# Block-sparse attention with a fused MLP: picked block numbers loaded one block at a time, and a new order table

## The chip, the cores and the metric

The kernel runs on one core of one Trainium2 chip. The metric is the device time of one execution in microseconds. TensorE multiplies matrices, VectorE (DVE) and ScalarE (ACT) do elementwise work, GpSimd (POOL) some of that and the indirect gathers, and SyncE (SP) issues most of the DMA transfers.

## The reference, cut to what matters

Block-sparse attention over 4 batches of 8 heads, 768 positions of 64 dimensions, in blocks of 32. A query block sees the blocks beside it, the first and the last block, and three blocks that an input picks for it. The attention output goes through a two-layer MLP.

```python
mask = np.abs(blk_i - blk_j) <= window
mask = mask | (blk_i == 0) | (blk_j == 0) | (blk_i == n_blocks - 1) | (blk_j == n_blocks - 1)
for qb in range(n_blocks):
    for kb in sampled_blocks[qb]:
        mask[qb * block:(qb + 1) * block, kb * block:(kb + 1) * block] = True
scores = np.where(mask, scores, -1000000000.0)
...
h = x @ w_in
relu6 = np.clip(h + 3.0, 0.0, 6.0)
g = h * relu6 / 6.0
return (g @ w_out).astype(np.float32)
```

## The kernel before, in words

**Units.** The attention is cut into 28 units, u0 to u27; a unit is four query blocks of one batch, for all eight heads. Its steps: `q` loads the queries; `keys` loads the eight key blocks of one query block (five neighbours in one transfer, three picked ones in one each); `values` loads four neighbours' values; `gather` fetches the picked values (an indirect DMA on GpSimd with the row numbers of the tile `rows`, or four plain transfers on SP). `s` (halves 0 and 1) makes scores on TensorE, `r_` reads them on VectorE with bias and row minimum, `e` is the exponential on ScalarE, `t` the transposes on TensorE, `c` copies them out of PSUM, `a` is the product with the values, `n_` the division on VectorE, `x` a transpose, and `xh` and `xl` split the result into a rounded part (ScalarE) and its residue (VectorE). The units of batch 0 that come first, u0 to u2, have their keys already on the chip (`keys0` of k0 loads a whole batch): for them `chosen` copies the three picked key blocks of one query block, with a picked number in a register as the address. The other units' `keys` and SP's `gather` take the numbers from registers of SP.

**MLP.** Three units make a chunk of 384 rows; eight chunks with 16 steps each are the steps m0 to m127. A step's `h` is twelve matmuls, `ga` and `gb` (ScalarE, VectorE) the activation, `gh` and `gl` its rounded part and residue, and `o0` to `o2` three matmuls each. 32 weight tiles w0 to w31 come in as 512 KB of 64-bit words each and are turned into float32 by `size`, `low` (ScalarE or another), `sign` and `bits` (VectorE), then split by `hi` and `lo` into rounded part and residue, again for every chunk. Nine buffers take the raw words; `load` into one waits for the `bits` of the weight that was there before.

**Order.** The order of everything is written out in a table, SCORE: every phrase names a unit, weight or step, and the operations to be issued next; a letter behind a point names the engine (d VectorE, a ScalarE, p GpSimd, s SP). Each engine runs its own operations strictly in that order, and so does SP with its transfers: a transfer whose buffer is not yet free holds up those behind it.

**The registers.** `registers` (line 383) loads, on the engine that asks, all 16 picked numbers of a unit at its first `chosen` (or `keys`) in one instruction, and the unit keeps them for that engine. The numbers lie in the tile `picked`, which VectorE clamps at the start. k0's `place` on TensorE and `rows` on VectorE make the gathers' row numbers; `flag`, `spread` and `bias` make the mask's bias.

Of the kernel before, what the change touches and what calls it, by code (L numbers as in the profile page):

```python
# [61 lines left out]
w11 bits; m4 ga; w15 load6; w16 size; m5 h; w12 bits; m3 gh.a; m4 gb; w5 hi.p; w7 hi.a; w12 hi.a; w13 sign; u4 keys0; w16 low.a; u3 s0; w5 lo.d; w12
lo.d; m2 o0; w14 low.a; u3 r_00; m3 gl.p; m6 h; w14 size; u3 r_01; u4 values0; w13 bits; u3 e00; w18 load0; u3 e01 r_02; w7 lo.p; m5 ga; u3 r_03 s1
e02; w22 load4; m5 gb; u3 e03; w14 sign; w20 load2; m2 o1; w15 size; u3 r_10; w15 low.p; w17 size; m3 o0; u3 r_11 e10; w14 bits; u4 keys2; m2 o2; u3
e11 r_12; w17 low.p; m3 o1; w14 hi.a; u3 r_13; m4 gh.a; u3 t00; w14 lo.d; w9 hi.a; u3 t01 t10; m4 gl.d; u3 e13; u5 q; m3 o2; u3 c01.a; w9 lo.d; u4
values1; u3 c10.a; m7 h; w21 load3; w15 sign; m6 ga; w16 sign; w11 hi.a; u3 e12; m6 gb; w19 load1; m5 gh.p; u3 c00.a; m4 o0; w16 bits; w18 size; u4
keys3; u3 t11; m5 gl.d; w16 hi.a; m4 o1; w15 bits; m7 ga; u3 c11.a; m4 o2; w16 lo.d; w20 size; m7 gb; u3 a; w11 lo.p; w13 hi.a; w20 low.a; w13 lo.d;
w22 size; m8 h; u4 keys1; u3 d; u4 gather3.p; w19 size; w17 sign; w21 low.a; u3 n_; w18 low.p; w22 low.a; m5 o0; w17 bits; u4 gather2.p; w19 low.a; u5
keys0; u3 x; m6 gh.d; w21 size; m5 o1; w20 sign; u5 gather0.p; u3 xh; m6 gl.d; m5 o2; u3 xl; m8 ga; u5 gather1.p; m6 o0; w20 bits; m7 gh.a; w15 hi.a;
m6 o1; m8 gb; u4 values2; m7 gl.d; u4 values3 s0; w25 load2; w15 lo.d; m6 o2; w18 sign; u5 values1; u4 r_00; m7 o0; m8 gh.a; w18 bits; u4 e00; u5  # L70
keys1; m7 o1; u4 r_01; w17 hi.a; m8 gl.d; u4 e01; m7 o2; u4 r_02; w17 lo.p; w18 hi.a; u4 r_03 t00 e02 s1 e03; w22 sign; w23 load0; u5 values0; u4
c00.a; w18 lo.d; m8 o0; w20 hi.a; u4 r_10; w25 low.p size; u4 t01 r_11; u6 q; m8 o1; u4 e10; w20 lo.d; u4 e11; m9 h; u4 r_12 c01.a; w22 bits; u4 e12;
u5 keys2; u4 r_13; w21 sign; u4 e13 t10; w23 size; w19 sign; m10 h; w22 hi.a; u4 d; w26 load4; u4 c10.a; w19 bits; m9 ga; w22 lo.d; w24 load1; w19
hi.a; u4 t11; m9 gb; m8 o2; m10 ga; w23 low.p; u4 c11.a; m10 gb; m11 h; m9 gh.a; w19 lo.d; m10 gh.a; w23 sign; u5 keys3; m9 gl.d; u4 a; w23 bits; m11
ga; w26 size; w21 bits; w26 low.a; m11 gb; w27 load0; w21 hi.p; m9 o0; u5 values2; u4 n_; w24 size; u5 values3 gather2.p; w24 low.a; w21 lo.d; u4 x;
m9 o1; m10 gl.d; u4 xh; u5 gather3.p; w24 sign; m10 o0; u4 xl; m9 o2; u6 gather2.p keys3; w24 bits; u5 s0; m11 gh.a; w25 sign; w23 hi.a; u6 gather3.p;
m10 o1; m11 gl.d; w24 hi.a; u5 r_00; w27 size; m10 o2; w24 lo.d; u5 e00; w28 load1; u5 r_01; w27 low.p; m12 h; u5 e01 r_02; w23 lo.d; u5 e02 r_03; w25
bits; u5 e03 s1; m12 ga; w26 sign; w29 load2; u6 keys2; m11 o0; m12 gb; w25 hi.p; u5 r_10; m12 gh.a; u5 t00; w25 lo.d; m11 o1; u5 e10 r_11 c00.a; m12
gl.p; m11 o2; w28 size; u5 r_12; u6 values3; w26 bits; u5 e11 t01; u6 values2; m12 o0; u5 e12 r_13; w28 low.p; w26 hi.a; u5 t10; w27 sign; u5 e13; m12
o1; u5 c01.a; w26 lo.d; u5 t11 c10.a; m12 o2; w27 bits; u5 c11.a; m13 h; w29 size; u5 d; w30 load0; w27 hi.a; w28 sign; w27 lo.d; u5 a; w28 bits; m13  # L80
ga; w29 low.d; w28 hi.a; w31 load1; m13 gb; w28 lo.d; u6 s0; m13 gh.a; u8 gather0.p; u6 values4; w30 low.a; u5 n_; m14 h; m13 gl.d; w30 size; u6 r_00;
w30 sign; u6 e00 r_01; w31 size; w30 bits; u5 x; u6 e01; m13 o0; u6 r_02; u5 xh; w31 sign; u6 t00; w30 hi.a; m13 o1; u6 r_03; w0 hi.a; w30 lo.d; m14
ga; m13 o2; u5 xl; u6 e02; m15 h; u6 c00.a; w0 lo.d; u6 e03; m14 gb; w29 sign; m14 gh.a; w31 low.d; m16 h; m15 ga; w29 bits; u8 keys2; w2 hi.a; m15
gb; w29 hi.a; w2 lo.d; m15 gh.a; u6 s1; w31 bits; w4 hi.a; m14 gl.d; w31 hi.a; u7 values5; m17 h; u6 r_10; w29 lo.p; m16 ga; u7 values6; u6 r_11 e10;
m16 gb; u6 e11 r_12; m14 o0; m15 gl.d; w6 hi.a; u6 r_13 e12 t01; u9 keys0; w31 lo.d; u6 t10; m17 ga; m14 o1; w4 lo.d; u6 e13; m15 o0; u6 c01.a; m17
gb; u6 c10.a; w6 lo.d; u6 t11; m15 oc0.a o1; u8 q; u6 d c11.a; u8 values0; m14 o2; m15 oc1.d od0; m19 h; m16 gh.a; m15 od1; w1 hi.a; m16 gl.d; w1
lo.p; m15 o2; u9 keys1; m16 o0; m17 gh.a; w3 hi.a; m18 h; m17 gl.d; w3 lo.p; m15 oc2.d; u8 keys0; m17 o0; m18 ga; m19 ga; m16 o1; m18 gb; w8 hi.a; w10
hi.p; m19 gb; u6 a; w8 lo.d; w10 lo.d; m15 od2; m17 o1; u6 n_; u8 gather2.p values3 values1; m16 o2; u8 values2 gather3.p; m21 h; u8 keys3; w5 hi.a;
m18 gh.a; w5 lo.d; u8 gather1.p; m18 gl.d; m17 o2; m20 h; w7 hi.a; m19 gh.a; w7 lo.d; m19 gl.d; u8 keys1; m18 o0; m20 ga; w12 hi.p; w14 hi.a; u7 s0;
# [688 lines left out]
```

## Time and profile before

| | |
|---|---|
| three runs | 779.84 us median (779.8 to 781.73) |
| profiled execution | 779.34 us; its span, from the first to the last instruction, is 777.6 us |
| mean granted TensorE clock | 0.995 |
| busy: TensorE, VectorE, ScalarE, GpSimd | 754.0, 520.9, 406.5, 187.3 us |
| DMA | 119.53 MB moved, mean 154 GB/s |

Times in the profile count from the first instruction of the span. Nearly all operations go through one helper, line 242, so a row is told apart by its tiles (output <- inputs) and its time. "Busy" of TensorE is modelled from pipelined matmuls. An idle time in front of an instruction is put down to what ended it; "issue" means that the profile shows nothing that the engine waited for.

### The profile page before, as it was taken

To read this page: it belongs to the slowest core of one execution; us is meant where nothing else is said; L and a number is where in the kernel's file an instruction comes from. 1 tells how busy PE (TensorE), PEld (TensorE's weight loads), DVE (VectorE), ACT (ScalarE), POOL (GpSimd) and SP (SyncE) were. 2 spreads that over 40 slices of the span, in tenths; PEclk is the share of its full clock that TensorE was granted. 3 is DMA by queue.
4 is the path that set the end of the run, shared out by engine and by line. 5 is a ranking of instruction groups with operands and counts; after the bars stand their busy time and mean duration, and the time that the engine had idled before them with its cause. 6 is when DMAs were issued, how large, how long until landed. Compare 5 with 4: busy or idle time off the path is not lost.

```text
span 777.6 us, 22739 instructions
## 1 busy us (share of the span) xinstructions
PE 754.0 (97%) x9078; PEld 649.8 (84%) x9078; DVE 520.9 (67%) x1304; ACT 406.5 (52%) x996; POOL 187.3 (24%) x200
## 2 busy tenths in 40 slices
PE   5789999999999999999999999999999999999996
PEld 5679887888888888898888888888888898889985
DVE  2568988955565665565656666767777677676763
ACT  2677977847555656455656553343543522452122
POOL 4531434141332221102123004222013511300110
PEclk9999999999999999999999999999999999999999
DMA  9949997660464673147245517464145670201001
GB/s 325 392 171 305 297 301 262 195 211 15 151 184 118 180 234 117 42 122 215 70 143 179 168 43 225 170 185 145 62 148 141 206 255 2 83 3 41 0 1 41
DMA packets 79687, 119.53 MB, mean 154 GB/s; under 512 B 10018, under 2 KB 45990, under 8 KB 79582
## 3 DMA queue, kind: packets, MB, share of 16 engines
q1 hardware_dynamic: 72674, 96.18, 38.6%
q0 software_dynamic: 6640, 21.76, 8.9%
q8 instruction: 72, 1.18, 0.6%
q14 instruction: 33, 0.27, 0.1%
q10 hardware_dynamic: 268, 0.14, 0.1%
...
## 4 chain that ended last, share of the span: by engine, by line
PE 89%; DVE 1%; DMA 0%; issue 0%; ACT 0%; ACTq 0%
PE out L242 35%; PE h L242 33%; PE att L242 21%; DMA out_dram<-ot 0%; DVE wout L242 0%; DVE wlo_in L242 0%; DVE wlo_out L242 0%; ACT ot L242 0%; DVE g L242 0%; DVE win L242 0%; ACTq L242 0%
## 5 line engine op out<-in xcount | busy, mean ns | idle before, releaser
L242 PE MATMUL h<-x,whi_in 128*128 128x384 f32 x1024 | 265.1, 339 | 1.7 <-ACT x L242 1.4
L242 PEld LDWEIGHTS h<-x,whi_in 128*128 128x128 f32 x1024 | 186.9, 189 | 12.3 <-ACT x L242 1.6
L242 PE MATMUL h<-x,wlo_in 128*128 128x384 f32 x512 | 172.9, 338 | 0.3 <-DVE wlo_in L242 0.3
L242 PE MATMUL out<-whi_out,ghi 128*128 128x512 f32 x384 | 162.2, 422 | 0.0
L242 ACT ACTIVATE p<-p,m 128x256 f32<-128x256 f32 x224 | 112.6, 504 | 83.8 <-DVE m L242 82.9
L242 PE MATMUL out<-whi_out,glo 128*128 128x512 f32 x384 | 151.6, 395 | 0.0
L242 PE MATMUL out<-wlo_out,ghi 128*128 128x512 f32 x384 | 151.1, 394 | 0.0
L242 ACT ACTIVATE g<-h,half_b 128x384 f32<-128x384 f32 x128 | 73.0, 580 | 149.2 <-PE h L242 131.6
L242 POOL DMA_INDIRECT vr<-vB,rows x77 | 76.9, 999 | 167.9 <-PE att L242 145.7
L242 DVE SCALAR_TENSOR_TENSOR g<-g,h 128x384 f32<-128x384 f32 x128 | 69.7, 551 | 57.8 <-ACT g L242 57.2
L242 PEld LDWEIGHTS h<-x,wlo_in 128*128 128x128 f32 x512 | 96.5, 188 | 0.6 <-DVE wlo_in L242 0.6
L242 PEld LDWEIGHTS out<-whi_out,ghi 128*128 128x128 f32 x384 | 72.2, 188 | 22.3 <-issue 12.3
L242 DVE TENSOR_TENSOR wlo_out<-wout,whi_out 128x512 fp32r<-128x512 f32 x106 | 76.1, 718 | 21.9 <-ACT whi_out L242 18.9
L242 DVE TENSOR_TENSOR wlo_in<-win,whi_in 128x512 fp32r<-128x512 f32 x107 | 75.2, 704 | 21.0 <-ACT whi_in L242 18.4
L242 DVE CUSTOM_DVE_ANT_1 p<-att,bias 128x256 f32<-128x256 f32 x176 | 68.6, 419 | 25.8 <-PE att L242 25.5
L242 PEld LDWEIGHTS out<-whi_out,glo 128*128 128x128 f32 x384 | 72.1, 188 | 16.3
L242 PEld LDWEIGHTS out<-wlo_out,ghi 128*128 128x128 f32 x384 | 72.5, 189 | 7.7
L242 DVE TENSOR_TENSOR glo<-g,ghi 128x384 fp32r<-128x384 f32 x114 | 67.9, 596 | 14.2 <-ACT ghi L242 12.0
L242 POOL TENSOR_TENSOR wlo_in<-win,whi_in 128x512 fp32r<-128x512 f32 x21 | 27.8, 1322 | 160.1 <-DVE whi_in L242 105.5
L242 ACT CAST ghi<-g 128x384 fp32r<-128x384 f32 x94 | 47.9, 512 | 32.1 <-PE out L242 29.4
L242 ACT COPY pt<-att 128x512 f32<-128x512 f32 x89 | 51.0, 586 | 24.6 <-PE att L242 23.7
L242 PE MATMUL att<-kr,q 64*32 64x256 f32 (+1 forms) x1280 | 59.7, 376 | 0.7 <-issue 0.7
...
## 6 DMA issues: line engine op xcount, KB each, us to landing
...
```

What stands on the lines that cost most here:

```text
L242: self.last = tc.keep_in_program_order(op(*a, **k)).ins
```

## The change

`registers` on an engine other than SP now loads the three numbers of one query block alone and keeps them with that block; SP still loads 16 for a unit. A new operation `numbers` does this load by itself, and the new table has twelve of them, all right behind the clamp: nine on ScalarE, three on VectorE. All twelve `chosen` remain; nine are on ScalarE and three on VectorE (before: four each on ScalarE, VectorE and GpSimd).

The table itself is made anew. It has the same operations otherwise, in another order, and some on other engines. Counts before and after: `hi` on ScalarE 127 and 256, on VectorE 112 and 0, on GpSimd 17 and 0; `lo` on VectorE 213 and 255, on GpSimd 43 and 1; `gh` on ScalarE 94 and 126, on VectorE 24 and 0, on GpSimd 10 and 2; `gl` on VectorE 114 and 99, on GpSimd 14 and 29; `c` on ScalarE 95 and 62, on VectorE 17 and 50; `oc` on ScalarE 13 and 24, on VectorE 11 and 0; `low` on ScalarE 18 and 28, on VectorE 4 and 2, on GpSimd 10 and 2; `gather` on GpSimd 83 and 82, on SP 5 and 6. `place` stands behind u0.s0 and no longer ahead of `spread`. The diff, the table cut to the part up to the first MLP steps:

```diff
 SCORE = """
-k0 load keys0; u0 q values1 values0 values2 values3; k0 clamp folding number flag; u0 chosen2.a; u1 q; u0 chosen0.p; k0 place; u1 values1 values0; u0
-chosen1.a chosen3.p; u1 values3 values2; k0 rows; u1 chosen0.p; k0 spread; u2 values1 values0; u1 chosen1.d; u0 gather0.p s0; u2 values3; k0 bias; u0
-gather2.p; w4 load4; u0 s1 r_00; w1 load1; u0 gather1.p e00 r_01; u2 values2; u0 e01 r_02; w0 load0; u0 gather3.p e02 r_03 t00 r_10; u2 q; u1
-chosen3.a; u2 chosen1.d; u1 gather1.p; w2 load2; u0 c00.a r_11; w3 load3; u0 e10 r_12; u1 chosen2.p; u0 e11 r_13 e12; u1 gather3.p; w6 load6; u2
-chosen0.d; u1 s0; u0 e03 e13; u1 gather0.p; u0 d t01; u1 r_00; w4 size; u0 t10; u1 gather2.p; w4 low.d; u1 e00; u0 t11 c01.d c10.a; u1 s1 r_01; u2
-gather2.p; u0 c11.a; w4 sign; u1 e01 r_02; w1 size; u2 gather1.p; w4 bits; u1 t00; u3 q; u1 e02 r_10 c00.a r_03; u2 gather0.p; u1 e10; w5 load5; u1
-r_11 e03; u2 chosen3.d; u0 a; u1 e11; u2 gather3.p; u1 r_12; u2 chosen2.a; w1 low.d; u1 r_13 e12; w1 sign; w0 size; u2 s0; u3 gather2.p; u0 n_; u1
-e13; u3 keys1; w0 low.a; w1 bits; w2 size; u1 d; u0 x; u2 r_00; w1 hi.p; w2 low.a; u1 t01; u2 r_01; u1 t10; u2 e00; u3 gather0.p; w2 sign; w8 load8;
-u1 t11 c01.a; u2 r_02 s1; u1 c10.a; w1 lo.d; w7 load7; u1 c11.a; u2 r_03 e02; w3 low.p; u2 e01; u1 a; u2 r_10; w6 low.p; u2 e03 r_11 e10; u3
-gather1.p; w2 bits; u0 xh; u2 e11 r_12; u0 xl; w3 size; w10 load1; u2 t00; u4 gather1.p; u1 n_; u2 e12 t01 c00.a r_13 t10; u4 gather0.p; u2 c01.a; w0
-sign; u1 x; u2 e13; w3 sign; u1 xh; u2 t11 d c10.a; u1 xl; u2 c11.a; w0 bits; w6 size; u2 a; w5 size; w3 bits; w9 load0; u3 keys2 gather3.p; w0 hi.a;
-w6 sign; w2 hi.a; w0 lo.d; w3 hi.a; u2 n_; w5 low.a; w2 lo.p; w8 low.a; u2 x; w12 load3; w6 bits; w8 size; u2 xh; w3 lo.d; w7 size; u2 xl; w11 load2;
-w7 low.a; w8 sign; m0 h; w7 sign; w10 low.a; u3 values2; w8 bits; w10 size; w7 bits; m1 h; w4 hi.a; w10 sign; m0 ga; w4 lo.d; w9 size; u3 values1; m0
...
+k0 load keys0; u0 q; u1 q; u0 values2 values3 values1; k0 clamp; u0 numbers3.a numbers1.a numbers2.a numbers0.d; u1 numbers0.a numbers1.a numbers3.d
+numbers2.a; u2 numbers1.a numbers0.d numbers3.a numbers2.a; k0 folding flag; u0 chosen3.a values0; u1 values0; u0 chosen1.a; u1 values3 values2; u0
+chosen2.a; u1 values1; u0 chosen0.d; k0 spread; u1 chosen0.a; w0 load0; k0 number; u1 chosen1.a; u2 values2; u0 s0; k0 bias; u2 values1 values0; k0
+place; u2 values3; u0 r_00 s1; k0 rows; w1 load1; u0 e00 r_01 gather1.p e01 r_02 e02 r_03 t00 gather3.p; u2 q; u1 chosen3.d chosen2.a; u0 r_10 e03; u1
+s0; u0 c00.d; w2 load2; u0 gather2.p e10; w6 load6; u0 r_11; u2 chosen1.a chosen0.d; u0 gather0.p e11 r_12 t01; w0 size; u1 r_00; u0 r_13 t10 e12; u1
+gather2.p; u0 c01.d; u1 s1; u0 e13; u1 r_01; u0 c10.a; u1 gather3.p; u0 d; u1 gather0.s e00 r_02 e01; u0 t11; w0 low.d; u1 gather1.p e02 r_10 t00; u2
+chosen3.a; u0 c11.d; u1 e10; u2 gather2.p; u1 r_11; u3 q; u2 chosen2.a; u1 c00.d; u0 a; u1 e11 r_12; u2 gather0.p; u1 r_03; w1 low.a; w7 load7; u1
+r_13 e12; w0 sign; u2 gather1.p; u1 e13; w0 bits; u1 e03; u2 s0 gather3.p; w1 size; u0 n_; w0 hi.a; u1 d; w4 load4; w2 size; u3 gather3.p; w1 sign; u0
+x; w2 low.a; u2 r_00; u1 t01; w1 bits; u0 xh; u3 gather1.p; u1 t10; u2 e00; u1 c01.d t11; w1 hi.a; w3 load3; u1 c10.d; u2 s1; u3 gather0.p; u1 c11.a;
+u0 xl; w6 size; u2 r_01; u3 keys1 gather2.p; w6 low.a; w0 lo.d; u2 e01 r_10 r_02 e10 r_11; u1 a; u2 e02 r_03 e11; u3 values2; u2 r_12 e03; w1 lo.d; u2
+e12 r_13; w8 load8; w7 size; w6 sign; u2 t00; u4 gather0.p; u2 e13; u1 n_; u2 t01; w7 low.a; u2 c00.d t10; u4 gather1.p; u2 c01.a d t11 c10.a; w6
+bits; u1 x; w5 load5; w4 low.a; u2 c11.d; u1 xh; w7 sign; u2 a; w4 size; u3 values3; u1 xl; w3 low.a; w4 sign; w3 size; w7 bits; w4 bits; u3 keys0; u2
+n_; w3 sign; u2 x; w2 sign; u2 xh; w3 bits; w8 low.a; u3 values0; u2 xl; w10 load1; w3 hi.a; u3 values1; w2 bits; w5 low.a; m0 h; w9 load0; w3 lo.d;
+w2 hi.a; w5 size; w2 lo.d; w8 size; w5 sign; m1 h; m0 ga; u3 keys2; w8 sign; w4 hi.a; m0 gb; w4 lo.d; m0 gh.a; w6 hi.a; w5 bits; m2 h; m1 ga; u4 q; m0
...
 """
...
@@ -370,6 +371,7 @@
 
         def __init__(self, unit, quad=None, third=None):
             self.unit, self.quad, self.third, self.on_chip = unit, quad, third, False
+            self.held = {}
             if third is None:
                 self.blk = GROUPS[unit.g][quad]
                 self.kn = len(k_items) % RING
@@ -382,14 +384,16 @@
 
         def registers(self, eng):
 
-            held = self.unit.held
+            o, n, at = 16 * self.unit.g, 16, 4 * self.quad
+            held = self.unit.held if eng is dma else self.held
+            if eng is not dma:
+                o, n, at = o + at, NR, 0
             if eng not in held:
-                o = 16 * self.unit.g
                 with tc.issue_after(eng.last):
                     _, held[eng] = nc.values_load_multi_w_load_instructions(
-                        picked[0:1, o:o + 16], engines=[eng.engine.engine], min_val=0, max_val=NB - 1,
+                        picked[0:1, o:o + n], engines=[eng.engine.engine], min_val=0, max_val=NB - 1,
                         skip_runtime_bounds_check_because="the numbers are clamped to 0 and 23 before")
-            return held[eng][4 * self.quad:4 * self.quad + NR]
+            return held[eng][at:at + NR]
 
         def chosen(self, eng):
             self.on_chip = True
@@ -458,6 +462,9 @@
         def q(self):
             self.Q = sb.tile([P, HP, P], F32, name="q")
             dma.dma_start(out=self.Q.rearrange("p h q -> p (h q)"), in_=qT[self.b, self.g])
+
+        def numbers(self, i, eng):
+            self.items[i].registers(eng)
 
         def chosen(self, i, eng):
             self.items[i].chosen(eng)
```

## Rows read from the trace of the kernel before

**Rows 1.** page, part 1: busy us, share of the span and instructions of each engine

```profile
PE 754.0 (97%) x9078; PEld 649.8 (84%) x9078; DVE 520.9 (67%) x1304; ACT 406.5 (52%) x996; POOL 187.3 (24%) x200
```

**Rows 2.** windows: stretch, length, busy us (count) PE PEld DVE ACT POOL, clock, DMA, GB/s

```profile
40.00:60.00 20.00, 16.01 (x422) 14.17 (x418) 14.58 (x36) 15.86 (x38) 5.38 (x5) 0.93 0.51 173
```

**Rows 3.** timeline of TensorE in the head: start, length, count [idle before <-what ended it]

```profile
33.69 1.21 PE L242 MATMUL out<-vr,pt 128*32 128x64 f32 x71 [2.05 <-issue]
38.95 0.29 PE L242 MATMUL out<-kn,q 64*32 64x64 f32 x1 [1.93 <-issue]
...
56.41 0.66 PE L242 MATMUL out<-ident,xs 128*128 128x128 f32 x4 [1.89 <-DVE xs L242]
59.18 0.44 PE L242 MATMUL h<-x,whi_in 128*128 128x384 f32 x1 [0.29 <-DVE x L242]
```

**Rows 4.** windows between TensorE's restarts, and one with idle DMA; columns as in rows 2

```profile
27.51:33.68 6.17, 4.12 (x127) 3.70 (x128) 3.32 (x16) 3.60 (x14) 1.93 (x2) 1.00 1.03 394
33.68:38.94 5.26, 3.33 (x128) 3.02 (x127) 1.57 (x4) 3.18 (x8) 3.21 (x5) 1.00 1.05 385
...
46.40:49.05 2.65, 2.65 (x147) 2.51 (x144) 1.80 (x8) 1.27 (x4) 0.00 (x0) 1.00 0.02 6
```

**Rows 5.** page, part 3: the instruction queue: packets, MB, share

```profile
q8 instruction: 72, 1.18, 0.6%
```

**Rows 6.** timeline of VectorE: u2.r_10, then u2.n_

```profile
47.25 0.42 DVE L242 CUSTOM_DVE_ANT_1 p<-att,bias 128x256 f32<-128x256 f32 x1 [3.24 <-PE att L242]
...
55.67 0.68 DVE L242 TENSOR_TENSOR xs<-att,m 128x512 f32<-128x512 f32 x1
```

**Rows 7.** tile picked, register loads on ScalarE: ns min/median/max, first and last start

```profile
L389 ACTq TENSOR_LOAD <-picked x3: 1020/1023/1216, 3.3 to 31.3; - x3
```

**Rows 8.** timelines of ScalarE, TensorE and VectorE at the start

```profile
6.75 1.28 ACT L242 ACT_TABLE_LOAD   x1 [6.75 <-DMA kn<-kN]
8.55 1.29 ACT L242 COPY kr<-kn 128x128 f32 x6 [0.52 <-DMA kn<-kN]
...
11.23 0.74 PE L242 MATMUL h<-kn,q 64*32 64x96 f32 x4
...
16.29 0.42 DVE L242 CUSTOM_DVE_ANT_1 p<-h,bias 128x256 f32<-128x256 f32 x1 [4.74 <-PE h L242]
```

**Rows 9.** timeline of GpSimd: the first and the fourth gather of u0

```profile
13.86 1.13 POOL L242 DMA_INDIRECT vr<-vB,rows  x1 [0.32 <-issue]
...
17.80 0.95 POOL L242 DMA_INDIRECT vr<-vB,rows  x1 [0.30 <-issue]
```

**Rows 10.** DMA issues: the gathers, count, median us from issue to landing

```profile
vr<-vB,rows POOLq DMA_INDIRECT x77, 4.7
...
wout<-vB,rows POOLq DMA_INDIRECT x3, 7.8
```

**Rows 11.** timeline of SP: u3.q, and w9.load0

```profile
30.13 0.33 SPq L242 DMA_DIRECT2D q<-qT  x1
...
53.74 0.33 SPq L242 DMA_DIRECT2D wraw<-w_out  x1
```

**Rows 12.** timeline of TensorE: m2.h, then m0.o0; m12.h, then u5.s1

```profile
64.84 0.51 PE L242 MATMUL h<-x,whi_in 128*128 128x384 f32 x2
...
66.92 0.39 PE L242 MATMUL out<-whi_out,ghi 128*128 128x512 f32 x1
...
124.54 0.51 PE L242 MATMUL h<-x,whi_in 128*128 128x384 f32 x2
...
126.75 1.09 PE L242 MATMUL att<-kr,q 64*32 64x256 f32 x32
```

**Rows 13.** timeline of TensorE: u12.s0 and u19.s0

```profile
288.19 1.56 PE L242 MATMUL att<-kr,q 64*32 64x256 f32 x32
...
480.50 1.72 PE L242 MATMUL att<-kr,q 64*32 64x256 f32 x32
```

**Rows 14.** page, part 5: roundings of weights on ScalarE, busy us, mean ns | idle before

```profile
L242 ACT CAST whi_in<-win 128x512 fp32r<-128x512 f32 x67 | 40.9, 617 | 16.8 <-PE h L242 16.8
```

More of the change, by code (lines that the diff above doesn't have):

```diff
@@ L62 @@
[L62 to L89, printed above, removed]
@@ new lines @@
+u3 keys3; m1 gl.d; w9 low.a; w8 lo.d; m0 o1; m3 ga; w9 sign; m1 o0; w12 size; m3 gb; m0 o2; w9 bits; w11 load2; w12 low.a; u4 values1; m1 o1; w12
+sign; w5 hi.a; w15 load6; m4 h; m2 gh.a; w10 bits; w14 size; m2 gl.d; w18 load0; w10 hi.a; w5 lo.d; w13 low.a; m1 o2; w10 lo.d; m4 ga; u4 keys0; u3
+s0; w13 size; w12 bits; m3 gh.a; m4 gb; w14 low.p; w7 hi.a; m2 o0; u3 r_00; w12 hi.a; w13 sign; m5 h; u3 e00; u4 values0; u3 r_01; w19 load1; w11
+low.a; w7 lo.d; w21 load3; u3 e01 r_02; w15 low.a; m3 gl.d; u3 s1; w16 load7; u3 r_03 e02; w14 sign; u3 e03 t00 r_10; m5 ga; u4 keys2; m3 o0; w12
@@ new lines @@
+lo.d; u3 e10 r_11; m2 o1; w15 size; u3 c00.d e11; m6 h; u3 r_12; w11 size; m5 gb; u3 e12; w17 load8; u3 r_13; u5 q; w18 size; w15 sign; m2 o2; u3 e13;
+w18 sign; w19 size; m3 o1; u3 d; w9 hi.a; u3 t01; w15 bits; m4 gh.a; m3 o2; u3 c01.a; u4 keys1; w9 lo.d; u3 t10; w16 size; m4 gl.d; u3 t11 c10.a; w14
+bits; m4 o0; u3 c11.a; m6 ga; w11 sign; u3 a; w14 hi.a; u4 keys3; m6 gb; m5 gh.a; w11 bits; w16 low.a; w14 lo.d; m4 o1; w11 hi.a; u4 gather2.p; u3 n_;
+w17 low.a; m7 h; w11 lo.d; w17 size; u4 gather3.p; w13 bits; w19 low.a; w20 load2; u4 values3; w16 sign; w18 low.a; u5 gather0.p; w22 load4; u3 x; m5
@@ new lines @@
+gl.d; u4 values2; w21 low.a; m4 o2; w16 bits; m7 ga; u5 gather1.p; m5 o0; m6 gh.a; w18 bits; u5 keys1; w13 hi.a; u4 s0; m7 gb; w16 hi.a; w13 lo.d; w18
+hi.a; m5 o1; u4 r_00; u3 xh; m6 gl.d; u4 e00; m5 o2; u4 r_01; w20 size; w16 lo.d; m6 o0; w15 hi.a; u4 r_02; m7 gh.p; m8 h; w20 low.a; u3 xl; m7 gl.p;
+u4 r_03 e01 e02; w20 sign; u4 e03 t00; w15 lo.d; w22 low.a; u5 keys0; u4 t01 c00.d; m7 o0; m8 ga; w18 lo.d; u4 c01.a s1; w22 size; m8 gb; w20 bits; m9
+h; u5 keys2; u4 r_10; w20 hi.a; w17 sign; u4 e10 r_11; w20 lo.d; u4 e11; m6 o1; u4 r_12; m9 ga; w17 bits; u4 t10 e12; m10 h; u4 r_13 c10.a; u5 keys3;
@@ new lines @@
+w19 sign; w21 size; m9 gb; u4 e13; w21 sign; u4 t11; w19 bits; m7 o1; w25 load2; u4 c11.d; m6 o2; w24 load1; w21 bits; u6 q; u4 a; m8 gh.a; w22 sign;
+w17 hi.a; m8 gl.d; w22 bits; m10 ga; m7 o2; u5 gather3.p; w17 lo.d; u6 keys3; w22 hi.a; u5 s0; m10 gb; m9 gh.a; u5 gather2.p; w19 hi.a; w22 lo.d; m8
+o0; w25 size; u5 r_00; w19 lo.d; w25 low.a; u6 gather2.p; m11 h; w26 load4; u5 r_01; w24 size; u5 values1; u4 d; w23 load0; w24 low.a; u5 r_02 values3
+e00; m9 gl.d; m8 o1; u4 n_; u5 e02; m11 ga; m9 o0; w24 sign; u5 e01; m11 gb; u4 x; w24 bits; u5 t00; u4 xh; m8 o2; u6 keys2 gather3.p; u5 r_03 c00.a;
@@ new lines @@
+u4 xl; m9 o1; w24 hi.a; w25 sign; w21 hi.a; u5 s1; m10 gh.a; w24 lo.d; w26 size; m9 o2; w21 lo.d; w28 load1; w26 low.a; u5 values0 r_10; m12 h; u5
+e03; w26 sign; u5 values2; w23 size; u5 r_11; m11 gh.a; m10 gl.d; w23 low.a; u5 r_12; m11 gl.p; m10 o0; m12 ga; u5 r_13 t01 e12; u6 values3; w23 sign;
+m10 o1; u6 values2; u5 e13; m12 gb; u5 e10; u6 s0; w23 bits; w28 size; u5 c01.d; w28 low.p; w27 load0; w23 hi.a; m10 o2; u6 r_00; u5 e11; w23 lo.d; u6
+e00; u5 t10; u6 r_01; m12 gh.a; m11 o0; w26 bits; u5 c10.a; u6 e01 r_02; m11 o1; m12 gl.p; w26 hi.a; u6 r_03; u5 t11; u6 e02; w28 sign; m11 o2; w27
@@ new lines @@
+low.a; w26 lo.d; u6 t00; w27 size; w28 bits; m13 h; u5 c11.a; w27 sign; w31 load1; w28 hi.a; u6 e03; w25 bits; u6 c00.a; w27 bits; u5 a; w29 load2;
+w25 hi.a; w28 lo.d; m13 ga; w30 load0; w27 hi.a; w25 lo.d; u6 s1; m13 gb; u8 gather0.p; w27 lo.d; w31 size; m14 h; m13 gh.a; u6 r_10; w31 sign; u6 e10
+r_11; w29 low.a; m13 gl.p; u6 r_12; w29 size; m12 o0; u5 d; w30 size; u6 r_13; w30 low.a; m13 o0; w29 sign; m14 ga; u5 n_; m12 o1; u6 e12; w30 sign;
+u5 x; u6 e11; m13 o1; m14 gb; u5 xh; w30 bits; u6 t01 e13; u5 xl; u6 t10; w30 hi.a; m12 o2; w29 bits; w0 hi.a; u6 t11 c10.a c01.d; m13 o2; u8 keys1;
```

270 lines of the change are left out of this document (137 added, 133 removed).

## The prediction

> **What bounds the kernel now.** The page comes first: TensorE is busy for 97% of the span, VectorE for 67%, ScalarE for 52%, GpSimd for 24% [rows 1]. With 754.0 of 777.6 us busy, at most 23.6 us can be won by anything that leaves TensorE's work as it is. The stretches show where a part of them lies: TensorE misses 4.0 us in 40 to 60, at a mean granted clock of 0.93 [rows 2]. From about 62 us on it hardly stops. So two things matter: when the first MLP group (m0.h) runs, and whether a new stall comes later.
>
> The waits of the head have two kinds. The timeline of TensorE shows a stop of 2.05 us inside u0.a and one of 1.93 us inside u2.s0 that nothing in the program ended ("issue") [rows 3]. Between the points at which TensorE came to life again (27.5, 33.7 and 38.9 us) the table of stretches counts 127 and 128 matmuls [rows 4]. The instruction queue moved 72 packets, 1.18 MB [rows 5]; TensorE runs 9078 matmuls and as many weight loads [rows 1], which is 252 instructions for each packet, or 126 matmuls. So I read the stops as TensorE at the end of its block of instructions, with the next still under way. A block took 6.2 and 5.3 us while the DMA engines were full (385 to 394 GB/s). In 46.4 to 49.05 us the DMA engines stood still (6 GB/s), and 147 matmuls ran in 2.65 us with no stop [rows 4]. The Trainium skill, "Runtime: NRT & Kernel Launch", section Instruction fetch mechanics, says that crossing a 16 KiB block is mostly hidden; the two stops show that here, under full DMA traffic, it is not. By that rule the head term below would be -0.4 us and not +1.8.
>
> The second kind is order: TensorE waits 1.89 us for u2.n_, and at m0.h for u2.xh and u2.xl, until 59.18 [rows 3]. VectorE and ScalarE have weight work queued ahead of these: u2.a ends at 56.41 - 1.89 = 54.5, u2.n_ starts at 55.67 [rows 6].
>
> **The register loads.** Before, ACT, DVE and GpSimd load 16 numbers at a time; on ACT a load took 1.02 to 1.22 us [rows 7]. After, ACT has nine loads of three numbers in a row, from 3.3 us, and DVE three, in time in which it waits for its tables anyway. Nothing shows a load of three numbers: its cost lies between 3/16 of 1.02 = 0.19 us and the full 1.02 us. No row tells a fixed price from one by the number, so I take the middle, 0.6. Then ACT is done at 3.3 + 9 x 0.6 + 0.2 = 8.9, the table load (1.28 us) ends at 10.2, and three copies for each of three blocks, at 0.2 us each (six in 1.29 us), end at 12.1. TensorE starts u0.s0 at 11.23 [rows 8] with the block that DVE copied, and by the pace of its 96 matmuls needs ACT's three at about 12.1, 12.6 and 13.2. Cost: nothing; the cover is spent at some 0.66 us a load. The Trainium skill, "DMA: Bandwidth & Descriptors", section Latency and other measured facts, gives about 600 ns as the floor of such a load; by that the sum stays the same.
>
> GpSimd loses its loads and its four copies, but the product that makes its row numbers now stands behind u0.s0, whose scores VectorE reads at 16.29 [rows 8]: the first gather moves from 13.86 to about 16.8 us, the fourth from 17.80 [rows 9] to 20.7. At the longer of the two medians from issue to landing, 7.8 us [rows 10], it is there at 28.5, and u0.a starts near 31: hidden.
>
> **The DMA order in the head.** Before, SP sends six weights (0.52 MB each) ahead of u3.q; after, only four, and one gather. Both times u3.q waits for the end of u1.s1, 30.1 [rows 11]. With 0.8 MB less ahead of it and gathers that start 3 us later, SP's queue is empty from about 26.5, and only gathers run until 30; the block that TensorE asks for at 27.5 can come sooner. That gains between 0 and 1.8 us (TensorE needs it at 31.9 at the earliest, and had it at 33.69); I take 1.0. The next block, again under full traffic, takes 5.3 to 6.2 us, say 5.75: 32.7 + 5.75 = 38.4, against 38.95. From there to the end of u2.s1, where VectorE starts to read it, are 47.25 - 38.95 = 8.3 us [rows 3, 6]: 46.7.
>
> Then comes what is lost. Before, SP stood until 53.74 [rows 11], because w9.load0 needs w0.bits, and the DMA engines ran dry: u1.a met no stop. After, w0 is unpacked early, and 7.9 MB come from u3.q on without a hold (weights 7, 4, 3, 8, 5, 10 and 9, four values and two keys of u3, seven gathers); at 393 GB/s that is 20 us, to 51. So the block asked for inside u2.s1 at 45.8 comes at 45.8 + 5.75 = 51.6, and u1.a ends at 51.9 and not 49.3. Behind it DVE has u1.n_, u2.c00, u2.d, w6.bits, u2.c11, w7.sign, u1.xl, w4.sign, w7.bits and w4.bits before u2.n_: nine of 0.6 us and one of 0.4, 5.9 us with what they wait for. u2.n_ 57.8, u2.x 58.6, u2.xh 59.2, three more weight operations, u2.xl done at 61.0. There m0.h's second product starts, against 59.18 [rows 3]: **+1.8 us**. Without that stop in u1.a DVE would still set the pace, by its own row from the end of u2.s1: 58.8, or -0.4. With the full 6.2 us at every block it is +3.6.
>
> **The order on TensorE.** Its instructions are the same, 9078 matmuls. A group h takes 2.08 us when out follows (64.84 to 66.92) and 2.21 when a score group follows (124.54 to 126.75) [rows 12]. By the order tables 18 groups h are followed by scores, attention products or a transposed x before, and 5 after: 13 x 0.1 = **-1.3 us**.
>
> **The stalls later.** u12.s0 and u19.s0 take 1.56 and 1.72 us [rows 13], against 1.09 for u5.s1 [rows 12]; u24.s0 pauses like them. With 0.5 to 0.8 us each they are 1.9 us, for keys that came late. Counted in TensorE's work between the issue and the use in the two tables, u19's and u24's last keys move ahead (from 7 and 6 us to 24 and 9), u12's come nearer (from 15 to 7), and eight more units have theirs some 7 us ahead. Bounds: 1.9 gained, or as much lost; I take half the gain, **-0.9**.
>
> **ScalarE, VectorE, GpSimd later.** All roundings of weights go to ScalarE (256, before 127), nearly all residues to VectorE (255, before 213); GpSimd keeps the gathers. ScalarE gains 129 x 0.62 us [rows 14] = 80 us on 406.5 [rows 1], some 63% of the span with the smaller moves: TensorE covers it. The tight place is the first MLP chunk: ahead of m8, ten of GpSimd's twelve weight and gate operations go to the other two, 6 to 7 us in some 35. I put nothing for this in the sum, and 1.5 us in rival 3.
>
> Sum: 1.8 - 1.3 - 0.9 = -0.4 us. The profiled execution took 779.34 us, 1.74 more than its span, so 778.9; the median of the three runs is 0.5 higher, so **779.4 us**.
>
> **The rivals.** (1) The blocks come sooner in the head: if neither u0.a nor u2.s0 stops, u2.s0 ends near 37, u1.a's block comes at 47.7, and m0.h's second product starts at 56.8: -2.4, in all 779.8 - 2.4 - 2.2 = 775.2 us. For it speaks the emptier queue at 27 us; against it, that SP fills the queue again from 30.1. (2) A register load costs its full price: ACT's loads end at 12.7, the table load at 14.0, the second block's copy at 15.2, so u0.s0 stops for 3.1 us, and all behind it is in order: 779.4 + 3.1 = 782.5 us, slower. It decides from 0.66 us a load on. For it speaks that every load took about 1 us; against it, that all had 16 numbers. (3) u1.a and u2.a both stop for a block at the long price, and ScalarE falls behind near m7: 779.8 + 3.6 + 1.5 - 2.2 = 782.7 us.
>
> **How the numbers follow.** What a measurement here can tell from no change is 0.3%, 2.3 us: 777.5 to 782.2. The forecast has 0.40 (most of it within, a part faster), rival 1 0.28, rival 2 0.18, rival 3 0.14. Faster: rival 1's 0.28 and 0.10 of the forecast, 0.38. Slower: most of rivals 2 and 3, 0.28. The same: 0.34. The range takes in rival 1 (775.2) and rivals 2 and 3 (782.7) with about 1 us beyond: 774.5 to 783.8. The forecast's own is 777 to 782.
>
> **What would show it.** ACT's nine loads done before 10 us, each about 0.6; u0.s0 with no pause of over 0.3 us; TensorE's stop in u0.a shorter than 2.05; a stop of 2 to 4 us inside u1.a with the DMA engines above 350 GB/s at 46 to 50; u2.xl done at about 61; u24.s0 near 1.1. The prediction is wrong where u1.a does not stop, where the nine loads reach past 10 us, or where TensorE pauses between m5 and m10.

## The result, and the profile after

After took 788.2 us in the median of five runs (785.49 to 789.26), before 779.84 beside it (779.35 to 781.73): a ratio of 1.0095, 95% interval 1.0072 to 1.0118. A second comparison gave 788.86 against 780.11, 1.0102 (1.0079 to 1.0124). So the change makes the kernel some 8.5 us slower, and I had forecast 779.4. The profiled execution took 788.34 us, its span 786.6. In two of the five comparisons below, before itself took 801.9 and 800.3 us: the profiles taken there show TensorE pausing within the first 54 us at many places where nothing in the program ended the pause (11 times in before_o, up to 1.2 us) and waiting longer for other engines later, so times of those are compared only within them.

The page's first part for after, to be read against [rows 1]:

```profile
PE 756.9 (96%) x9078; PEld 652.9 (83%) x9078; DVE 494.3 (63%) x1212; ACT 486.4 (62%) x1160; POOL 116.4 (15%) x127
```

ScalarE went where I had put it (406.5 + 80 = 486.5). TensorE runs the same 9078 matmuls in nearly the same busy time; what was added is time in which it stands. The head comes first, TensorE's timeline of after against [rows 3]:

```profile
32.74 2.15 PE L243 MATMUL out<-vr,pt 128*32 128x64 f32 x71 [2.04 <-issue]
39.15 0.24 PE L243 MATMUL out<-kn,q 64*32 64x64 f32 x1 [1.61 <-issue]
...
52.94 0.22 PE L243 MATMUL att<-wout,pt 128*32 128x64 f32 x1 [4.06 <-issue]
...
61.39 0.66 PE L243 MATMUL out<-ident,xs 128*128 128x128 f32 x4 [2.03 <-DVE xs L243]
62.72 0.45 PE L243 MATMUL h<-x,whi_in 128*128 128x384 f32 x1 [0.68 <-ACT x L243]
63.79 0.69 PE L243 MATMUL h<-x,whi_in 128*128 128x384 f32 x1 [0.63 <-DVE x L243]
```

The stop in u0.a is as long as before (2.04 against 2.05). The stop in u1.a is new, 4.06 us. The wait for u2.n_ stands behind it nearly unchanged (2.03 against 1.89), and m0.h's second product starts at 63.79 against 59.18: 4.6 us are lost in the head. The stretches of after around u1.a, columns as in [rows 4]:

```profile
46.17:50.16 3.99, 2.71 (x126) 2.41 (x127) 3.02 (x14) 2.49 (x11) 0.00 (x0) 1.00 0.94 255
50.16:52.94 2.78, 0.00 (x0) 0.00 (x0) 0.34 (x1) 1.76 (x5) 0.00 (x0) 1.00 0.91 265
53.24:56.65 3.41, 3.41 (x35) 3.24 (x24) 2.28 (x5) 0.84 (x2) 1.89 (x2) 0.50 1.01 320
```

From 46.17 TensorE has one block of instructions left, 126 matmuls. The packet with the next one starts only at 50.16 in the trace, while the DMA engines are 94% busy, and the first matmul of that block starts 2.78 us later. In before, the same packet started at 46.44, 0.05 us after TensorE had entered its last block, with the engines at 2% [rows 4], and there was no stop.

The third row is a smaller loss that came with the stop: right behind the 4.06 us in which TensorE stood, its granted clock is 0.50, the lower level of 1.2 GHz. Before has the higher level from 42.4 to 59.5 us. VectorE waits 0.30 and 0.72 us there for u2's transposes and takes 6.95 us from u1.n_ to u2.n_, against 6.18 before.

The last group of three matmuls starts at 780.07 us, before at 770.59: 9.5 us later, so 4.9 of them are lost behind m0.h. There TensorE's timeline of after shows two things that the forecast had not. First, score groups that take 1.5 us and not 1.09 [rows 12] (1.45 and 1.02 when counted to the start of the next group, as below):

```profile
391.19 1.99 PE L243 MATMUL att<-vr,pt 128*32 128x64 f32 x128
393.11 1.52 PE L243 MATMUL att<-kr,q 64*32 64x256 f32 x32
```

That is u14.a and then u15.s0. Second, pauses that nothing in the program ended, as in u12.a:

```profile
322.95 1.97 PE L243 MATMUL att<-vr,pt 128*32 128x64 f32 x123
325.48 0.31 PE L243 MATMUL att<-vr,pt 128*32 128x64 f32 x5 [0.56 <-issue]
```

I numbered TensorE's instructions of the built program (a weight load and a matmul each count one, a semaphore instruction one) and looked up at which number every such pause of over 0.1 us stands. In the twelve profiles used here for times there are 88, and **all 88 stand at instruction 193 or 194 of a block of 256**; 256 is also 18,442 instructions over the 72 packets of [rows 5]. So they are the ends of blocks. This holds for these twelve; in the other eight, of the comparisons in which before took 800 us and more, TensorE also pauses inside blocks in the first 54 us, and why is not known. The sums over the twelve, from the traces, in us:

```
kernel          ahead of 62 us   behind
before               4.73         0.42
after                8.52         3.00
after_again         12.22         3.76
head_before          5.84         2.74
head_after           7.89         1.02
sp_held              5.89         2.59
phase_3              7.96         1.85
between_7            6.84         2.50
best_before_2        5.65         1.08
regs16              10.86         3.24
o_between_3          7.25         2.91
best_after           4.68         0.75
```

### The profile page after: what moved, and what is told of

It reads as the page before. It is cut to its first block, busy times and chain, and to the rows that moved or that the text cites. A ratio compares the mean times of both kernels' runs of the same rounds, so it can differ in the third digit from the quotient of the medians.

```text
span 786.6 us, 22710 instructions
## 1 busy us (share of the span) xinstructions
PE 756.9 (96%) x9078; PEld 652.9 (83%) x9078; DVE 494.3 (63%) x1212; ACT 486.4 (62%) x1160; POOL 116.4 (15%) x127
## 4 chain that ended last, share of the span: by engine, by line
PE 94%; issue 2%; DVE 1%; DMA 1%; ACT 1%; ACTq 0%
PE out L243 36%; PE h L243 35%; PE att L243 23%; DMA p<-spread 1%; DVE wout L243 1%; DMA out_dram<-ot 0%; ACT p L243 0%; ACTq L243 0%; DVE p L243 0%; DVE win L243 0%; DVE xs L243 0%; ACT ot L243 0%; DVE x L243 0%; DVE pt L243 0%; ACT wraw L243 0%
## 5 line engine op out<-in xcount | busy, mean ns | idle before, releaser
L243 POOL DMA_INDIRECT vr<-vB,rows x76 | 74.1, 975 | 326.3 <-PE att L243 300.2
L243 DVE TENSOR_TENSOR wlo_in<-win,whi_in 128x512 fp32r<-128x512 f32 x128 | 88.2, 694 | 50.3 <-ACT whi_in L243 50.0
L243 DVE TENSOR_TENSOR wlo_out<-wout,whi_out 128x512 fp32r<-128x512 f32 x127 | 90.1, 709 | 29.6 <-ACT whi_out L243 28.6
L243 ACT CAST whi_in<-win 128x512 fp32r<-128x512 f32 x128 | 78.0, 616 | 41.3 <-PE h L243 40.3
L243 ACT CAST whi_out<-wout 128x512 fp32r<-128x512 f32 x128 | 79.1, 618 | 19.5 <-PE out L243 17.9
L243 ACT CAST ghi<-g 128x384 fp32r<-128x384 f32 x126 | 64.1, 511 | 31.0 <-PE out L243 28.3
L243 POOL TENSOR_TENSOR glo<-g,ghi 128x384 fp32r<-128x384 f32 x29 | 31.3, 1080 | 280.9 <-ACT ghi L243 244.5
L243 DVE TENSOR_TENSOR glo<-g,ghi 128x384 fp32r<-128x384 f32 x99 | 54.8, 555 | 26.9 <-ACT ghi L243 26.2
```

The costliest lines, as they stand in the source:

```text
L243: self.last = tc.keep_in_program_order(op(*a, **k)).ins
```

## The experiments

**Halves of the table.** Both order tables hold the same operations, so the head of one can be followed by the rest of the other. head_before is before's table to m2.h and after's from there; head_after the reverse.

```diff
 (head_before: the table of before)
 ...
 m2 h;
-(the rest of before's table)
+(the operations still missing, in after's order)
```

> Order table of before as far as m2.h, after's from there on; register loads as before (16 numbers). Computes the reference in full. Theory (two losses that have nothing to do with each other: about 4.6 us in the head, where u1.a stops for a block of instructions, and about 4.9 us net later, after m2.h): the head's loss is gone and the later one is all there, 779.8 + 4.9 = 784.7 us (784.0 to 785.5). Rival A (everything that is lost later follows from the late head, so it goes with it): 779 to 780. Rival B (all of the loss is in the order table behind m2.h): 788.

> Order table of after as far as m2.h, with its loads of three numbers, before's table from there on. Computes the reference in full. Theory: the head's loss alone, 779.8 + 4.6 = 784.4 us (783.5 to 785.4), with the stop of about 4 us inside u1.a in its trace and m0.h starting at about 62.7. Rival A: 787 to 788. Rival B: 780.

Measured beside 779.88: head_before 783.53 us (1.0052, 1.0032 to 1.0072), head_after 783.4 us (1.0045, 1.0029 to 1.0061). Rivals A and B fall: each half loses by itself, 3.65 and 3.5 us. That is about 1 us less each than one profile had told, and together 7.2 of some 8.5 us.

**The stop in u1.a.** Removed from after by letting SP stand, and made in before by more traffic.

```diff
 (sp_held: after)
 w5 load5;
+u4 q;
 w4 low.a; u2 c11.d; u1 xh;
 ...
-u4 q;
 m0 gl.d; w10 low.a; w12 load3;

 (before_dma: before)
 w10 load1;
+w5 load5; w8 load8; w7 load7; w10 load1;
+w5 load5; w8 load8; w7 load7; w10 load1;
```

> After, with one word of the table moved: u4.q stands right behind w5.load5 on SP's queue and so holds that queue, from about 40 us, until u2.s1 is done (about 46.8). Computes the reference in full. Theory (u1.a's stop of 4.06 us is TensorE waiting for its block of instructions behind the full data queues): the queues run dry at about 45, the block comes, u1.a does not stop, a stop of up to 1 us may come in u2.a when SP has filled the queues again: m0.h at about 59.5 and 788.2 - 3 = 785.2 us (784.3 to 786.3). Rival (the stop has nothing to do with the traffic): it stays at 4 us and the time at 788 or above, since weights and keys come later.

> Before, with eight more transfers of 0.52 MB on SP's queue behind w10.load1: the weights 5, 8, 7 and 10 are loaded three times to the same place instead of once, so that the data queues stay full from 37 to about 52 us. Computes the reference in full. Theory (the block of instructions that u1.a needs is asked for at about 46.4 us, and waits behind whatever data is queued): a stop of 2 to 5 us inside u1.a, at its matmul 104, where before has none, and 779.9 + 3 = 783 us (782 to 785). Rival (the stop in after belongs to its order of work and not to the traffic): no stop, within 0.3% of before.

sp_held took 784.1 us (1.0059, 1.0044 to 1.0074), 4.1 us less than the 788.2 of after. Its timeline of SP, then a stretch while TensorE runs its last block (columns as in [rows 4]), then the stop in TensorE's timeline:

```profile
42.03 0.33 SPq L243 DMA_DIRECT2D win<-w_out  x1
46.51 0.33 SPq L243 DMA_DIRECT2D q<-qT  x1
```

```profile
45.66:48.05 2.39, 2.39 (x126) 2.10 (x121) 1.73 (x11) 1.20 (x5) 0.00 (x0) 1.00 0.30 113
```

```profile
49.32 0.22 PE L243 MATMUL att<-wout,pt 128*32 128x64 f32 x1 [1.26 <-issue]
```

SP stands from 42.4 to 46.5, the DMA engines fall to 30%, the packet starts at 46.79 and the stop is 1.26 us. I had expected no stop in u1.a, so 1.26 us stay. The same transfers, only later, give 4.1 us back, a little more than the 1.9 to 3.9 expected: most of the stop is the traffic. before_dma was timed where before took 801.9 us: 803.92 us, 1.0021 (1.0004 to 1.0039), 2 us more. In that comparison's profiles u1.a stops for 3.06 us with the extra transfers, within the 2 to 5 expected, and for 0.87 us without them (in before_o). The whole gained just less than the 2.1 us at the lower end of what I expected; the direction holds.

The stop varies from one execution of after's head to the next: 4.06 (after), 5.43 (after_again), 5.43 (regs16), 3.56 (head_after), 2.14 (o_between_3), 1.87 (phase_3), 0.71 (between_7). In these seven the packet starts 0.7 (between_7) to 5.4 us (regs16) after TensorE enters its last block. Why it does so at such different times was not settled.

**The register loads.**

```diff
-            held = self.unit.held if eng is dma else self.held
-            if eng is not dma:
-                o, n, at = o + at, NR, 0
+            held = self.unit.held
 ...
-u0 numbers3.a; u0 numbers1.a; u0 numbers2.a; u0 numbers0.d;
 ...
```

> After's table without its early register loads, and the register loads of before: 16 numbers for each unit and engine, at the first use. Computes the reference in full. Theory (the register loads lie ahead of everything that sets the time and their cost ends at TensorE's first wait for instructions): u0.s0's matmuls take about 4.9 us and not 5.44, and the time is that of after within 0.5 us, 787.7 to 788.7. Rival (the nine loads at 0.70 us on ScalarE are a part of the head's loss): 1.5 to 3 us faster, 785.5.

(The twelve `numbers` operations are out of the table.) 787.5 us (1.01, 1.0083 to 1.0117): as after, the rival falls. What is lost comes with the new order table, not with the loads. The loads of after, on tile `picked` (ns min/median/max, first and last start), for [rows 7]:

```profile
L393 ACTq TENSOR_LOAD <-picked x9: 697/705/887, 3.5 to 26.5; - x9
L393 DVEq TENSOR_LOAD <-picked x3: 744/751/994, 2.2 to 16.7; - x3
```

A load of three numbers takes 0.70 us on ScalarE where one of 16 takes 1.02: mostly a fixed price. u0.s0 did not get shorter in regs16, as I had expected (5.9 us from its start to the next group, 5.4 in after and 4.65 in sp_held with the same loads), so its pace does not come from the loads.

**Scores behind attention products.** In after nine score groups with keys to wait for follow an attention group directly, in before five, and u12.s0, u19.s0 and u24.s0 are among before's five. o_between moves an MLP group in between; between_7 leaves u8 and u17 as they are; before_o does it in before.

```diff
 (o_between, one of nine)
-m56 o0;
 ...
 u14 a;
 ...
+m56 o0;
 u15 s0 r_00 e00;
```

> After, with nine words of the order table moved: for u8, u10, u15 to u19, u24 and u25 the group o of the MLP that stood just ahead of the attention products a (one or two groups ahead) stands between a and the scores s0 that followed a directly. No instruction is added. Computes the reference in full. Theory (a score group takes 1.43 us and not 1.02 when it follows an attention group directly, because TensorE's queue then meets the seven or so extra semaphore instructions of the score group late, and hides them behind any MLP group): each of the nine goes to 1.02, 9 x 0.4 = 3.6 us less, less 0.5 for what comes to stand elsewhere: 788.2 - 3 = 785.2 us (784.4 to 786.3). Rival (these units' keys come late): the nine stay at 1.4 or lose the same time elsewhere, 787.5 to 789.

> Before, with the same move for its five score groups that follow an attention group directly (u6, u12, u13, u19, u24). Computes the reference in full. Theory: 0.08 + 0.48 + 0.17 + 0.63 + 0.62 = 2.0 us less, 779.9 - 1.9 = 778.0 us (777.2 to 778.9). Rival (late keys, as I had it in the prediction): 779.9 within 0.5 us.

> The kernel of o_between again, since before itself took 801.9 us in that comparison and not 779.9. Theory and rival as there: 785.2 us (784.4 to 786.3) with the nine score groups at 1.02 us, against 787.5 to 789.

> The kernel of before_o again, for the same reason. Theory 778.0 us (777.2 to 778.9), rival 779.9 within 0.5 us.

> After, unchanged, to stand beside o_between and phase in one comparison. If before takes some 780 us, 788.2 us as first measured; if before again takes some 801 us, then longer than before by more than 1.0%, since after keeps the data queues full for longer while TensorE asks for its blocks.

> The kernel of o_between, beside after. Theory (scores straight behind attention products pay for their semaphore instructions): 3 us less than after in the same comparison (2 to 4). Rival (late keys): within 1 us of after.

> After, with the move of o_between for seven of the nine units only: u8 and u17 are left as they are, since there the moved group was the last to read a rounded weight, ScalarE could round the next one only 2.6 us later, and VectorE came so late to u6's and u16's part that TensorE waited 1.3 and 1.6 us for it. Theory (scores straight behind attention products cost 0.4 us each, and o_between lost what it gained in those two waits): 788.6 - 7 x 0.4 = 785.8 us (784.8 to 787.0). Rival (what is gained there is given back somewhere else whatever is moved): 787.5 to 789.

The first two pairs ran where before took 801.9 and 800.3 us: 826.42 and 822.85 for o_between (1.0312 and 1.0283), 802.96 and 804.34 for before_o (1.0011, 0.9994 to 1.0028; 1.0043, 1.0026 to 1.006). They don't size the cause, but before_o shows no gain, against my theory. In its trace u12.s0 does go from 1.50 to 1.02 us, but the moved group was the last to read a rounded weight: ScalarE waits 3.81 us for it, VectorE 3.74 us for ScalarE, and TensorE 1.79 us for VectorE ahead of u11.x, at 309.80, a wait that before_dma with the old order does not have. And u19.s0 and u24.s0 stay at 1.71 and 1.47 us, and the end of a block now lies inside each. o_between_3, beside 788.86 for after, took 788.05: 0.8 us less and not 3. In its trace six of the nine groups do go to 1.02 or 1.03 us and u24.s0 to 1.19, and the two other moves, at u8 and u17, bring a new wait. The timelines of ScalarE, VectorE and TensorE of o_between_3 at u17:

```profile
428.26 0.62 ACT L243 CAST whi_out<-wout 128x512 fp32r<-128x512 f32 x1 [2.94 <-PE out L243]
...
428.92 0.69 DVE L243 TENSOR_TENSOR wlo_out<-wout,whi_out 128x512 fp32r<-128x512 f32 x1 [3.99 <-ACT whi_out L243]
...
430.00 0.69 DVE L243 TENSOR_TENSOR xs<-att,m 128x512 f32<-128x512 f32 x1
...
430.83 0.63 PE L243 MATMUL att<-ident,xs 128*128 128x128 f32 x4 [1.57 <-DVE xs L243]
```

The moved m60.o2 is the last reader of a rounded weight. ScalarE now rounds the next one later (in after it waited 0.81 us there), VectorE stands behind its residue with u16.n_ queued, and TensorE waits for that; u8 has the same with 1.30 us. Without these two, between_7 took 785.35 us (1.0069, 1.0044 to 1.0094), 2.9 us less than 788.2 (3.5 less than 788.86): that agrees with 7 x 0.4, though the intervals of the two ratios are some 2 us wide to either side. In the two traces the seven groups take 11.35 and 7.87 us, 3.5 less, of which half a microsecond may be the block that ends in u24.s0 (2.47 and 1.74); the other six are at 1.02 or 1.03. Its rows at the same place as above, m56.o0 and u15.s0:

```profile
387.92 1.99 PE L243 MATMUL att<-vr,pt 128*32 128x64 f32 x128
389.85 0.50 PE L243 MATMUL out<-whi_out,ghi 128*128 128x512 f32 x1
...
390.75 1.09 PE L243 MATMUL att<-kr,q 64*32 64x256 f32 x32
```

Why it takes 1.5 us behind an attention group I read from the semaphore instructions of u15.s0 (seven in both kernels, each 51 ns; start times in us from the trace):

```
after      392.77 392.88 393.01 393.11 393.24 393.37 393.47   s0's matmuls from 393.11
between_7  389.53 389.64 389.77 389.88 390.00 390.13 390.29   s0's matmuls from 390.75
```

None of them lasts longer than 51 ns, and the DMA engines moved nothing from 384.2 to 392.9 us in after, so the keys had landed; but the seven follow each other at 0.1 us and more. With an MLP group in between, TensorE's queue reaches the first of them 1.22 us ahead of the scores and works through all of them while the three long matmuls run; straight behind an attention group it reaches the first only 0.34 us ahead, and matmuls of the scores wait for the later ones. The number of such instructions decides, and not the place behind attention alone: of the score groups straight behind one in before and after (u24.s0, with the end of a block in it, left out), those with none to two take 1.02 or 1.03 us, with three 1.10 and 1.19, with five 1.24, with seven 1.43 to 1.50, with eight 1.46 and 1.65, with nine 1.66.

**The borders of the blocks.** phase puts 80 instructions ahead of u2.x, so that every border behind it falls 80 instructions earlier in the program.

```diff
         def x(self):
             self.xt_ps = bank(self.first)
+            if self.n == 2:
+                for _ in range(20):
+                    pe.matmul(self.xt_ps[:32, :8], lhsT=ident[:32, :32], rhs=ident[:32, :8], start=True, stop=True)
             xs = self.xs.rearrange("p h d -> p (h d)")
```

> After, with 20 tiny matmuls (80 instructions on TensorE's queue) ahead of u2.x, where TensorE waits 2 us for u2.n_ anyway. They write a corner of the bank that u2.x writes over. Computes the reference in full. Theory (the pauses that nothing ended, behind u3.s0 too, are the borders of blocks of 256 instructions, and cost where two borders come within some 2.9 us): the pauses at matmul 125 of u3.a, ahead of m24.o0, at 123 of u12.a, 127 of u22.a and 24 of u24.s0 (3.0 us together) are gone; what pauses there are stand 80 instructions earlier in the old count, of which u8.s0, u16.s0, u17.s0 and u24.a come within 2.6 us of the border before. Time 786 to 788.5, since new pauses may take a part of the gain. Rival (those groups wait for data): the five pauses stay where they are, and the time at 788.2 to 789.

> The kernel of phase again, for the same reason. Theory: pauses behind u3.s0 stand only at the borders of the shifted blocks, 786 to 788.5 us. Rival: the five pauses stay where they are in after, 788.2 to 789.

> The kernel of phase, beside after. Theory (the pauses behind u3.s0 are the borders of blocks of instructions): those at u3.a, m24.o0, u12.a at matmul 123, u22.a and u24.s0 are gone, others stand only at borders of the shifted blocks, and the time is 0 to 2 us below after. Rival: the pauses stay where they are in after.

Where before took 801.9 and 800.3 us: 826.0 and 820.63 us, which says nothing of the size. phase_3 took 785.32 us (1.007, 1.0049 to 1.0091), 3.5 us less than after beside it, more than the 0 to 2 expected. The five pauses of after are gone. TensorE's timeline of phase_3, at u12.a and u22.a:

```profile
319.80 1.41 PE L244 MATMUL att<-vr,pt 128*32 128x64 f32 x83
322.15 0.87 PE L244 MATMUL att<-vr,pt 128*32 128x64 f32 x45 [0.94 <-issue]
...
591.63 1.99 PE L244 MATMUL att<-vr,pt 128*32 128x64 f32 x128
```

In u12.a the pause moved from matmul 123 to matmul 83, by the 40 loads and 40 matmuls put in; u22.a runs through. So they are borders and not data. Of the places that I had named for new pauses (u8.s0, u16.s0, u17.s0, u24.a) none paused; u12.a, m39.o1 and m11.h did. Behind 62 us the pauses fell from 3.0 to 3.8 us (after, after_again) to 1.85; that explains 1.2 to 1.9 of the 3.5 us. In the profiles the rest lies in the head, where m0.h's second product starts at 60.69 us against 63.79 (after) and 66.42 (after_again): u1.a stops for 1.87 us, and the wait for u2.n_, in which the new instructions run, is 0.21 us and not 2.03. Since the head differs from one execution to the next, how much of that the shift brought stays open.

**All together.** best_before is before_o with u2.n_, u2.x, u2.xh and u2.xl moved ahead; best_before_2 has only the moves that bring no wait; best_after joins sp_held, between_7, a shift by 80 instructions and the earlier u2.n_.

```diff
 (best_before_2: before)
 w2 hi.a;
+u2 n_ x;
 w0 lo.d; w3 hi.a;
-u2 n_;
+u2 xh;
 w5 low.a; w2 lo.p;
+u2 xl;
 w8 low.a;
 ...
-u2 x;
 ...
-u2 xh;
 ...
-u2 xl;
 ...
 (m44 o0 behind u12 a, m71 o2 behind u18 a, m92 o1 behind u23 a)
```

> Before with the five moves of before_o, and in the head u2.n_, u2.x, u2.xh and u2.xl moved ahead of the weight operations that stand in front of them on VectorE and ScalarE (w0.lo, then w5.low and w8.low). Computes the reference in full. Theory (TensorE's waits of 1.89 us for u2.n_ and at m0.h are the order of VectorE's and ScalarE's queues): u2.n_ starts 0.8 us earlier, u2.xl is done 1.4 us earlier, 778.0 - 1.3 = 776.7 us (775.8 to 777.8). Rival (m0.h or m1.h then waits for w0.lo or w2.lo instead): as before_o, 778.

> Before with a group o moved between attention products and scores for u13, u19 and u24 (not u6 and u12, where it delays a rounding of a weight or brings nothing), and with u2.n_, u2.x, u2.xh and u2.xl ahead of the weight operations as in best_before. Computes the reference in full. 780.0 - 0.2 - 0.4 - 0.6 - 0.9 = 777.9 us (776.8 to 779.2), faster than both kernels. Rival (the early u2.n_ only moves the wait to m1.h, and u24.s0 waits for a block anyway): within 0.5 us of before.

> After with all that the runs point to: u4.q ahead on SP's queue (sp_held), the seven moves of between_7, 20 tiny matmuls ahead of the spread (in time in which TensorE waits for its first data) that shift the borders of the blocks, and u2.n_, u2.x, u2.xh and u2.xl ahead of weight operations of VectorE. Computes the reference in full. 784.1 (sp_held) - 2.8 (seven score groups) - 1.0 (borders behind m2.h, as phase) - 1.2 (u2.n_ earlier) = 779.1 us (777.5 to 781.0). Rival (u1.a's stop comes back in another form, since the borders in the head are shifted too): 781 to 784.

best_before ran where before took 800.3 us: 803.58, 1.0039 (1.0024 to 1.0054), slower and not 3 us faster, with the same wait ahead of u11.x as before_o. **best_before_2 took 777.56 us beside 779.9, 0.9966 (0.9952 to 0.998), where 777.9 was expected, and is faster than both kernels.** The timeline of TensorE of best_before_2, at u2.x, m0.h's second product and m2.h:

```profile
56.14 0.66 PE L242 MATMUL out<-ident,xs 128*128 128x128 f32 x4 [0.99 <-DVE xs L242]
...
58.20 0.44 PE L242 MATMUL h<-x,whi_in 128*128 128x384 f32 x1 [0.29 <-DVE x L242]
...
63.61 0.62 PE L242 MATMUL h<-x,whi_in 128*128 128x384 f32 x2 [1.14 <-DVE g L242]
```

The wait for u2.n_ is 0.99 us against 1.89 [rows 3], as reckoned; a part comes back ahead of m2.h. best_after took 782.0 us (1.0026, 1.0008 to 1.0044), 3 us above what I expected and in the range of its rival: the gains don't add. In its profile u1.a does not stop, but u2.s0 does for 3.99 us; TensorE still waits 1.89 us for u2.n_, and 1.28 us at 130.23 for ScalarE, which waited 1.39 us for a weight.

## Why the prediction was wrong, by its steps

- **"The stalls later", -0.9 us: this step failed, in its cause and its sign.** I took u12.s0, u19.s0 and u24.s0 for late keys and counted the lead of the keys in both tables. They are scores with six to eight semaphore instructions straight behind attention products: with an MLP group in between, u12.s0 goes from 1.50 to 1.02 us (before_o), and u19.s0 from 1.65 to 1.25 and u24.s0 from 1.87 to 1.39 (best_before_2), the end of a block lying in both. The question for the two tables would have been how often such an s0 follows a: five times before, nine times after. In the two traces these groups take 2.0 and 4.1 us more than 1.02 each, borders left out. The second cause, the borders, I had read in the head only; behind 62 us they cost 0.42 us before and 3.0 to 3.8 after. Together that is +4.7 us in the first pair of profiles where the sum had -0.9. That the borders cost more in after because more attention groups stand next to scores is my reading; between_7, with seven of these pairs parted, still loses 2.50 us at them. The half by itself, head_before, lost 3.65 us, the order's gain already taken off.
- **The head, +1.8 us: the mechanism was right, the size not.** u1.a stopped where I said it would, at the end of a block and because w9.load0 no longer holds SP. I had priced the block at 5.75 us with 6.2 as the upper bound; from 46.17 to 52.94 it took 6.77, and up to 8.1 in after_again, with the DMA engines 94% busy at 255 GB/s where I had looked for above 350. u0.a went on at 32.74, where I had put it, but by luck: its stop was no shorter and its block took 6.3 us, as before (6.2), and TensorE had only entered the block ahead of it 1.07 us earlier. u1.n_ started at 53.70 and not 51.9, VectorE took 6.95 us from there to u2.n_ and not 5.9, and u2.xl ended at 63.74 and not 61.0; head_after alone lost 3.5 us. The Trainium skill's rule that I weighed there ("Runtime: NRT & Kernel Launch", section Instruction fetch mechanics) is that crossing a block is mostly hidden. By count the traces agree, with pauses at 5 to 9 of some 71 crossings in an execution; under traffic, and in groups of small matmuls, they don't, as the 88 pauses at the crossings show.
- **The register loads, nothing:** right in the time (regs16), but not by the sum that I gave. One took 0.70 and not 0.6 us, above the 0.66 at which I had the cover spent. The nine do not run in a row, as I had assumed: two run at 3.5 to 5.2 us and the others between the copies, the last from 26.5 us on, and u0.s0 started at 10.84 us, 0.4 earlier than before.
- **The order on TensorE, -1.3 us:** no run tried it alone. Summed over the median paces of neighbouring groups behind m0.h, the two traces differ by some 1.0 us in after's favour, which agrees with the sign and most of the size.
- **ScalarE, VectorE and GpSimd later, nothing:** ScalarE's load was met (486.4 us) and covered, but VectorE is late in places (0.63 us ahead of u5.x), some 1 us that I had in rival 3 alone.
- **The rivals.** Rival 3 (stops in u1.a and u2.a at the long price) came nearest with 782.7; u2.a did not stop, and it lacked nearly all that is lost behind m2.h. Rival 1 and rival 2 did not happen. Range and chances rested on the bound of 1.9 us for the later stalls, which holds only for a cause that I had not shown.
